# Hash attention and a squared-ReLU MLP: the last pair of the last chunk made a wide pair, gates moved to ScalarE, steps in another order

## The chip, the cores and the metric

One Trainium2 chip, one core of it. The metric is device time in microseconds (us) of the whole kernel, lower is better. All data are float32.

## The reference

Attention over 4 batches x 8 heads, 768 tokens, head size 64, in which a query sees only the keys of its own hash bucket (6 sign bits), followed by an MLP with a squared ReLU on the 3072 tokens:

```
mask   = bucket(q)[:, :, :, None] == bucket(k)[:, :, None, :]
attn   = softmax(where(mask, q @ k.T / 8, -1e9));  y = attn @ v
x      = y.transpose(0, 2, 1, 3).reshape(3072, 512)
h      = x @ w_in            # 512 -> 2048
g      = maximum(h, 0) ** 2
result = g @ w_out           # 2048 -> 512
```

## The kernel before

The first 310 us are the attention; beside it the weights are cut up and summed. Nothing of it is changed. The MLP then runs over three chunks of 1024 tokens (`i` = 0, 1, 2; the last is `NCHUNK - 1`), each with a first layer (`hidden...`) and a second (`project`). Both layers save multiplications with Winograd's form of Strassen's scheme: a product of two 2x2 block matrices is made of seven block products ("11", "21", "t1", "t2", "t3", "22", "t4") and some fifteen block sums.

The first layer of chunks 1 and 2 goes by pairs `n` = 0..3. A pair makes the 512-token columns of two rows of hidden blocks, `r0 = n` (upper) and `r = NQ + n` (lower), in the four quarters `b11`, `b12`, `b21`, `b22`; it runs as a left half (`half` 0) and a right half (`half` 1). Two forms are in use:

- `hidden_wide` (pairs 0 to 2): per half only the outer products "11" and "t2" are made whole, with 128x512 moving operands. The other five outer products, called A, D (left half), B, C, E (right half), are each cut again into seven products of 128x256 (`inner_steps`, whose `step_0` to `step_3` hold 2, 2, 2 and 1 of them).
- `hidden_pair` (pair 3): per half four outer products are whole ("11", "t1", "t2", "t3") and only A, B and C are cut again.

A float32 product is two matmul instructions on TensorE. After the products, VectorE adds the parts and either it makes the gate (`gated`, one instruction: max with 0 times itself) or ScalarE does (`gate_in`, two: Relu and Square). ScalarE also carries the products out of PSUM: `keep(acc, "one")` and `keep(acc, "two")` of the whole products, and the copies within `inner_steps`. "t2" is accumulated onto the bank that holds "11", so it can be written only after `one` was copied; in the same way each later step of A to E waits for the copy or the add that reads its bank before.

The order of all instructions is written by hand and every engine takes its own in that order (`tc.manual_schedule`). Work of a pair that is not due yet (gates, sums for the second layer) is put into the list `behind_pair` and called by `behind(m)` at fixed places of the next pair. PSUM: `acc0`, `acc1`, `acc2` with two buffers each and the two side banks `last0`, `last1`; before, the fourth product of A to D goes to a side bank.

Other names: `sums_inner` makes the right-hand sums of the cut products; `inner_sums(k)` those of the second layer's k-th outer product; `mark()` squares and adds up 768 elements per partition on ScalarE (32 such pieces, for a check of the inputs' size); `load_leaf` loads factors of the second layer (`leaf`, seven buffers), five of them ahead of `project`, on ScalarE's queue in chunks 1 and 2; `load_unit` loads the first layer's factors on SyncE's.

`project(i)` makes seven outer products k = 0..6 of seven inner ones each, all of 128x256, through `product`. In it `b11 = b22 - b_t` is made after k = 0 and `b_t = b21 - b11` after k = 2, each as two instructions of 128x2048.

Of the kernel before, what the change touches and what calls it, by code (L numbers as in the profile page):

```python
# [34 lines left out]
def kernel(  # L35
# [686 lines left out]
    def load_unit(n, pool=p_i):  # L722

        if n < NCHUNK * NR and n not in w_unit:
# [3 lines left out]
            if n < NR or pair == NQ - 1:  # L728
# [9 lines left out]
            if n >= 2 * NR:  # L738
                nc.sync.dma_start(out=five_six(w), in_=w_in_49[pair, :, 3 + half])
# [4 lines left out]
    def sum_unit(n):  # L744


        if NR <= n < 2 * NR and n % NR < NR - 2:
# [6 lines left out]
            nc.gpsimd.dma_start(out=w_in_49[pair, :, 3 + half], in_=five_six(w))  # L754
# [15 lines left out]
    with tc.manual_schedule():  # L770
# [201 lines left out]
        def product(n, w, at, bt, c11, c12, c21, c22, hook=None, last=False, beside=None, cuts=1):  # L972
# [16 lines left out]
            def keep(of, name):  # L989
                t = p_r.tile([P, 512], FP32, name=name, bufs=KEPT[name])[:, 0:w]  # L990
                nc.scalar.copy(out=t, in_=acc[of])  # L991
                return t
# [121 lines left out]
        w_inner, t_inner, spots, snaps, now, behind_pair = {}, {}, {}, {}, {}, {}  # L1114
# [77 lines left out]
        def sums_inner(i, js):  # L1192

            for j in js:
                y11, y12, y21, y22 = quarters_x(i, j)
                if j < 3:
                    tile = p_y.tile([P, NQ, QN], FP32, name=f"t{j}", **({"bufs": 2} if j < 2 else {}))
                    t = [tile[:, m] for m in range(NQ - 1)] + [y12]
                    spots[i, j] = tile[:, NQ - 1]
                else:  # L1200
# [3 lines left out]
                t_inner[i, j] = t  # L1204
# [5 lines left out]
        def inner_steps(i, j, side, w):  # L1210

            t1, t2, t4, t3 = t_inner[i, j]
            y11, _, y21, y22 = quarters_x(i, j)
            if i not in snaps:
                snaps[i] = [side_bank(m)[:, 0:QN] for m in range(2)]
            one = three = spots[i, side]
            hs = {}

            def new(unit):
                name = "five" if (j, unit) == (3, 0) else "three" if j == 4 else None
                if name:
                    return p_r.tile([P, 512], FP32, name=name, bufs=KEPT[name])
                return new_h()

            def mul(out, a, b, start, stop):
                nc.tensor.matmul(  # L1228
                    out=out, lhsT=w(a), rhs=b, start=start, stop=stop, skip_group_check=True
                )  # L1230

            def step_0():
                a0, a1 = (
                    ps_m.tile([P, 512], FP32, name=f"acc{m}")[:, 0:QN] for m in (0 if j == 4 else 1, 2)
                )
                mul(a0, 0, y11, True, False)
                nc.scalar.copy(out=one, in_=a0)
                mul(a1, 1, y21, True, True)
                hs[0] = new(0)
                nc.vector.tensor_tensor(out=hs[0][:, 0:QN], in0=a1, in1=one, op=ALU.add)  # L1240
                hs["a0"] = a0

            def step_1():
                last = hs["last"] = (
                    ps_m.tile([P, 512], FP32, name="acc2")[:, 0:QN] if j == 4 else snaps[i][side]
                )
                mul(hs["a0"], 4, t2, False, False)
                nc.scalar.copy(out=hs[0][:, QN:HN], in_=hs["a0"])
                mul(last, 3, t1, True, False)
                hs[1] = new(1)  # L1250
                nc.scalar.copy(out=hs[1][:, QN:HN], in_=last)

            def step_2():
                mul(hs["a0"], 5, t3, False, False)
                nc.scalar.copy(out=three, in_=hs["a0"])
                mul(hs["last"], 6, y22, False, True)

            def adds():
                for unit, by in (0, hs["last"]), (1, three):
                    add_in(hs[unit][:, QN:HN], by)  # L1260

            def step_3():
                mul(hs["a0"], 2, t4, False, True)
                nc.scalar.copy(out=hs[1][:, 0:QN], in_=hs["a0"])

            def put(unit, out, other):
                add_in(hs[unit], other)
                gated(out, hs[unit])

            return step_0, step_1, step_2, step_3, put, adds, hs  # L1270
# [43 lines left out]
        def hidden_wide(i, n, half):  # L1314

            r0, r = n, NQ + n
            w, acc, add, keep = outer_steps(i, n, half)
            own = own_factors(w, half)
            if half == 0:
                load_inner(i, n + 1)  # L1320
                load_third_inner(i, n + 1, nc.sync)
                now["A"] = inner_steps(i, 0, 0, w_inner[i, n][0])
                if n == 0:
                    sums_inner(i, (3,))
                now["D"] = inner_steps(i, 3, 1, lambda a: own[a])
            A, D = now["A"], now["D"]
            u0 = D[6]
            add(acc, 0, "11", True, False)
            one = keep(acc, "one")
            if half == 0:  # L1330
                A[0]()
                D[0]()
                if n == 0:
                    mark()
                    sums_inner(i, (4,))
                behind(0)
            else:
                B, C = inner_steps(i, 2, 0, w_inner[i, n][2]), inner_steps(i, 1, 1, w_inner[i, n][1])
                E = inner_steps(i, 4, 2, lambda a: own[a])
                B[0]()  # L1340
                C[0]()
                E[0]()
                A[4](1, b11[:, r], one)
                behind(2)
                sum_unit(i * NR + 2 * n + 2)
            add(acc, 4, "t2", False, True)
            two = keep(acc, "two")
            if half == 0:
                A[1]()
                D[1]()  # L1350
                A[2]()
                D[2]()
                A[3]()
                D[3]()
                if n == 0:
                    mark()
                A[5]()
                D[5]()
                add_in(u0[0], two)
                A[4](0, b11[:, r0], one)  # L1360
                sum_unit(i * NR + 2 * n + 1)
                behind(1)
                now["two"] = two
                return
            two_0 = now["two"]
            B[1]()
            C[1]()
            add_in(u0[1], two)
            B[2]()
            C[2]()  # L1370
            B[5]()
            E[1]()
            C[5]()
            B[3]()
            E[2]()
            B[4](0, b12[:, r0], u0[0])
            C[3]()
            E[3]()
            E[5]()
            B[4](1, b12[:, r], u0[1])  # L1380
            hC, hE = C[6], E[6]
            add_to(b22[:, r0], u0[0], hE[0])
            add_to(b22[:, r], u0[1], hE[1])
            add_in(two_0, hE[0])
            add_to(b21[:, r0], hC[0], two_0)
            behind(3)

            def step_0():
                gate_in(b22[:, r0])
                add_in(two, hE[1])  # L1390
                add_to(b21[:, r], hC[1], two)
                for m in r0, r:
                    minus(b_t[:, m], b12[:, m], b11[:, m])
                inner_sums(0, slice(n, n + 1))
                minus(b12[:, r0], b22[:, r0], b12[:, r0])

            def step_1():
                gate_in(b22[:, r])

            def step_2():  # L1400
                gate_in(b21[:, r0])
                minus(b12[:, r], b22[:, r], b12[:, r])

            def step_3():
                gate_in(b21[:, r])

            for m, step in enumerate((step_0, step_1, step_2, step_3)):
                behind_pair[m].append(step)

        def hidden_pair(i, n, half):  # L1410
# [3 lines left out]
            if half == 0:  # L1414
                now["A"], now["C"], now["B"] = (
                    inner_steps(i, j, (0, 0, 1)[j], w_inner[i, n][j]) for j in range(3)
                )
# [6 lines left out]
            else:  # L1424
                B[2]()
                B[5]()
                C[0]()
                A[4](1, b11[:, r], one)
                B[4](0, b12[:, r0], now["two"])
                behind(3)  # L1430
            other = ps_m.tile([P, 512], FP32, name="acc2")
# [13 lines left out]
            if half == 0:  # L1445
                A[2]()
                A[5]()
                B[0]()
                A[4](0, b11[:, r], one)
                add_in(two, five)  # L1450
            else:
                C[2]()
                C[5]()
                add_in(two, five)
                B[4](1, b12[:, r], two)
                minus(b_t[:, r], b12[:, r], b11[:, r])
                inner_sums(0, slice(n, n + 1))
                C[4](0, b21[:, r0], now["three"])
# [8 lines left out]
            else:  # L1467
# [3 lines left out]
                C[4](1, b21[:, r], three)  # L1471
# [95 lines left out]

        def project(i):
# [60 lines left out]
            for k in range(7):  # L1629
# [23 lines left out]

                def hook():
                    y21 = b[:, NQ:NR, 0:QN]
                    minus(y21, y21, t2)
                    if marks(i, k):
# [9 lines left out]
                    if k == 6 and more:  # L1667
                        load_third_inner(i + 1, 0, nc.scalar)
                        sums_inner(i + 1, (0, 1))

                counted = []

                def a_with_load(m, k=k):
# [4 lines left out]
                use = uses[k]  # L1678
                product(
                    NQ, QN, a_with_load, bt, lambda *p: use(0, *p), lambda *p: use(1, *p),  # L1680
                    lambda p: use(2, p, None), lambda *p: use(3, *p), hook,
                    (i, k) == (NCHUNK - 1, 6), mark if marks(i, k) else None,
                )
# [5 lines left out]
                if k == 0:  # L1689

                    for h in range(2):
                        at_h = slice(h * NQ, (h + 1) * NQ)
# [293 lines left out]
```

## Time and profile before

| | |
|---|---|
| median of 3 runs | 849.79 us (848.64 to 850.54) |
| profiled execution: own time / span | 851.49 us / 849.9 us |
| TensorE (PE) busy | 841.6 us, 99% |
| VectorE (DVE) busy | 758.5 us, 89% |
| ScalarE (ACT) busy | 439.8 us, 52% |
| granted TensorE clock | 0.999 |
| attention | 0 to 314 us |
| chunk 1: first layer / second | 495 to 585 / 585 to 670 us |
| chunk 2: first layer / second | 670 to 759 / 759 to 844 us |

An engine is busy from the start to the end of its instructions; matmuls are pipelined, so that the starts of successive ones (0.215 us apart) lie closer than their length (0.379 us). In a row of the timeline stand the start in us, the length, the engine, the line of the kernel, the operation and the tiles; a bracket names the idle time before it and what ended it. Line numbers in rows are those of the kernel before.

### The profile page before, as it was taken

To read this page: it belongs to the slowest core of one execution; us is meant where nothing else is said; L and a number is where in the kernel's file an instruction comes from. 1 tells how busy PE (TensorE), PEld (TensorE's weight loads), DVE (VectorE), ACT (ScalarE), POOL (GpSimd) and SP (SyncE) were. 2 spreads that over 40 slices of the span, in tenths; PEclk is the share of its full clock that TensorE was granted. 3 is DMA by queue.
4 is the path that set the end of the run, shared out by engine and by line. 5 is a ranking of instruction groups with operands and counts; after the bars stand their busy time and mean duration, and the time that the engine had idled before them with its cause. 6 is when DMAs were issued, how large, how long until landed. Compare 5 with 4: busy or idle time off the path is not lost.

```text
span 849.9 us, 17478 instructions
## 1 busy us (share of the span) xinstructions
PE 841.6 (99%) x6698; PEld 555.4 (65%) x6698; DVE 758.5 (89%) x1087; ACT 439.8 (52%) x833; POOL 171.0 (20%) x289
## 2 busy tenths in 40 slices
PE   9999999999999999999999999999999999999997
PEld 4444444444475445544788877767888777768885
DVE  4898999999999988989899989988988988888876
ACT  5887777878777762222211146775232457753210
POOL 1321121303221201643121220001211300021103
PEclk9999999999999999999999999999999999999999
DMA  9966999989996426999977994418878964157666
GB/s 185 201 130 138 185 186 201 207 173 224 249 245 202 158 69 245 330 312 306 359 254 220 275 226 145 146 50 292 298 214 244 247 207 145 51 169 213 201 166 128
DMA packets 237304, 174.10 MB, mean 205 GB/s; under 512 B 165224, under 2 KB 195248, under 8 KB 237216
## 3 DMA queue, kind: packets, MB, share of 16 engines
q1 hardware_dynamic: 196976, 90.14, 43.3%
q0 software_dynamic: 16992, 44.02, 16.5%
q10 hardware_dynamic: 23248, 38.78, 14.7%
q8 instruction: 54, 0.88, 0.5%
q14 instruction: 34, 0.28, 0.1%
HBM read 129.51 MB, written 42.73 MB: 203 GB/s over the span
## 4 chain that ended last, share of the span: by engine, by line
PE 95%; DMA 2%; DVE 1%; ACTq 0%; issue 0%; ACT 0%; POOL 0%; SPq 0%; POOLq 0%; DVEq 0%
PE acc L984 40%; PE st L478 18%; PE xo L532 14%; PE acc L1228 10%; PE acc L1298 8%; PE last L1228 3%; PE tot L589 1%; PE hash L396 1%; DMA bits<-signed 1%; DMA out_dram<-h 1%; PE tp L342 0%; DMA qk_nat<-in_q_dram 0%; ACTq L1499 0%; DVE h L1522 0%; DVE o L1288 0%
## 5 line engine op out<-in xcount | busy, mean ns | idle before, releaser
L484 ACT ACTIVATE e<-st 128x768 f32<-128x768 f32 x192 | 155.5, 810 | 56.8 <-PE st L478 52.5
L532 PE MATMUL xo<-e,v_nat 64*64 64x385 f32 (+1 forms) x1520 | 156.7, 483 | 0.0
L984 PE MATMUL acc<-b,leaf 128*128 128x256 f32 x600 | 133.1, 379 | 0.0
L984 PEld LDWEIGHTS acc<-b,leaf 128*128 128x128 f32 x600 | 113.9, 190 | 16.1 <-issue 0.5
L478 PE MATMUL st<-feat 64*64 64x384 f32 x1056 | 109.3, 483 | 0.0
L444 POOL DMA_DIRECT2D bits<-signed x120 | 62.1, 522 | 196.5 <-ACT signed L433 194.7
L532 PEld LDWEIGHTS xo<-e,v_nat 64*64 64x64 f32 (+1 forms) x1520 | 58.5, 133 | 65.7 <-issue 54.7
L984 PE MATMUL acc<-t,leaf 128*128 128x256 f32 x336 | 76.1, 379 | 0.0
L984 PEld LDWEIGHTS acc<-t,leaf 128*128 128x128 f32 x336 | 63.7, 190 | 9.1 <-issue 0.3
L478 PE MATMUL st<-bits 64*64 64x384 bf16 x768 | 65.9, 324 | 0.4 <-DMA bits<-signed 0.4
L520 DVE TENSOR_TENSOR total<-total,e 128x1536 f32<-128x1536 f32 x32 | 56.0, 1750 | 7.6 <-ACT e L484 6.9
L1028 POOL DMA_DIRECT2D raw_qk<-in_q_dram x32 | 17.3, 541 | 212.3 <-ACT raw_qk L1033 209.8
L520 DVE TENSOR_TENSOR t_x<-t_x,e 128x1536 f32<-128x1536 f32 x32 | 55.8, 1744 | 3.9 <-ACT e L484 3.8
L478 PEld LDWEIGHTS st<-feat 64*64 64x64 f32 x1056 | 39.8, 133 | 25.6 <-issue 21.7
L984 PE MATMUL acc<-x,w_unit 128*128 128x512 f32 (+1 forms) x144 | 56.5, 546 | 0.0
L984 PE MATMUL acc<-b_t,leaf 128*128 128x256 f32 x240 | 53.8, 379 | 0.0
L991 ACT COPY two<-acc 128x256 f32<-128x256 f32 (+1 forms) x29 | 12.5, 431 | 75.2 <-PE acc L984 59.7
L1076 DVE SCALAR_TENSOR_TENSOR b<-h 128x512 f32<-128x512 f32 x72 | 49.1, 691 | 2.2
L991 ACT COPY one<-acc 128x256 f32<-128x256 f32 (+1 forms) x29 | 12.5, 431 | 72.6 <-PE acc L984 53.3
L984 PEld LDWEIGHTS acc<-b_t,leaf 128*128 128x128 f32 x240 | 45.6, 190 | 6.2
L478 PE MATMUL st<-t_x 64*64 64x384 f32 x480 | 48.9, 482 | 0.0
L478 PEld LDWEIGHTS <-bits 64*64 64x64 bf16 x768 | 24.6, 107 | 35.2 <-issue 32.8
(234 smaller groups left out, 1537.8 us busy)
## 6 DMA issues: line engine op xcount, KB each, us to landing
leaf<-w_out ACTq DMA_DIRECT2D x142, 256.0 KB, 3.4
raw<-in_moe_w_in_dram SPq DMA_DIRECT2D x8, 1024.0 KB, 6.4
raw<-in_moe_w_out_dram SPq DMA_DIRECT2D x8, 1024.0 KB, 7.5
w_unit<-w_in SPq DMA_DIRECT2D x8, 896.0 KB, 8.5
w_out<-sums POOLq DMA_DIRECT2D x16, 448.0 KB, 7.4
v_nat<-in_v_dram SPq DMA_DIRECT2D x16, 384.0 KB, 5.1
x_all<-x_raw SPq DMA_DIRECT2D x16, 384.0 KB, 3.2
raw_qk<-in_q_dram POOLq DMA_DIRECT2D x32, 192.0 KB, 3.6
```

What stands on the lines that cost most here:

```text
L396: nc.tensor.matmul(out=banks[g * NR_B:(g + 1) * NR_B, h, 0:HS], lhsT=projs[rows, h * D:h * D + NR_B], rhs=feat[pr][rows, w, c * HS:(c + 1) ...
L444: nc.gpsimd.dma_start(out=t[h * D:h * D + NBITS + 1, w, c * HS:(c + 1) * HS], in_=signed[pr % 2][at:at + NBITS + 1, h],)
L478: nc.tensor.matmul(out=st[k * HK:(k + 1) * HK, h, 0:HS], lhsT=src[1][rows, key], rhs=src[0][rows, cut], start=first, stop=not first, skip_ ...
L484: nc.scalar.activation(out=key_of(pr, kt)[:, :, i, 0:HS], in_=st[:, :, 0:HS], func=ACTF.Exp, scale=scale)
L520: nc.vector.tensor_tensor(out=totals[pr], in0=totals[pr], in1=e, op=ALU.add)
L532: return nc.tensor.matmul(out=outs[pr][h * D:(h + 1) * D, c, 0:HS + 1], lhsT=nat[pr, "v_nat"][rows, h, kt * D:(kt + 1) * D], rhs=key_of(pr ...
L984: nc.tensor.matmul(out=acc[to][:, at_c], lhsT=a(i), rhs=b(i)[:, at_c], start=first and i == 0, stop=last and i == n - 1, skip_group_check= ...
L991: nc.scalar.copy(out=t, in_=acc[of])
L1028: nc.gpsimd.dma_start(out=raw_qk[i][:, w], in_=flat[:, i * n:(i + 1) * n])
L1076: nc.vector.scalar_tensor_tensor(out=out, in0=h, scalar=0.0, in1=h, op0=ALU.max, op1=ALU.mult)
L1228: nc.tensor.matmul(out=out, lhsT=w(a), rhs=b, start=start, stop=stop, skip_group_check=True)
L1298: nc.tensor.matmul(out=to, lhsT=w[:, PLACE[a], f], rhs=bt[b](f), start=first and f == 0, stop=last and f == NFT // 2 - 1, skip_group_check ...
```

## The change

- Last chunk: pair 3 is made by `hidden_wide` too (`i > 1 or s // 2 < NQ - 1`). Its factors are loaded in the wide form, and `sum_unit` makes the sums of its factors in place. What it leaves to do is not put into `behind_pair` but into `now["edge"]`: the first product (k = 0) of the last `project` calls it behind its own steps (`hook`, `early`, and `then` after the copies `two`, `five`, `three`). Three `mark()` that were in `hidden_pair` stand in its right half.
- Upper left gates: `b11[:, r0]` and `b11[:, r]` of wide pairs are gated by ScalarE (`gate_in`), and `b12[:, r]` in chunk 1 as well; before, VectorE did it (`put`).
- Steps in another order: in left halves of pairs 1 to 3, A's and D's first steps stand before "11" and their first three before "t2"; in right halves E's second step stands before C's third, and so on. `behind_pair` has six places in place of four, filled otherwise. The inner products use `acc1` and `acc2` alone (A to D) or the two side banks (E), and the second products' parts are added from PSUM on VectorE onto a copy.
- The five first leaves of chunks 1 and 2 are loaded by SyncE.
- `b11 = b22 - b_t` and `b_t = b21 - b11` are made by quarters: one quarter at the place of before, one in the hook of k = 2 and of k = 4, two in the hook of k = 3 and after k = 4.

The core of the diff:

```diff
-                (hidden_wide if s // 2 < NQ - 1 else hidden_pair)(i, s // 2, s % 2)
+                (hidden_wide if i > 1 or s // 2 < NQ - 1 else hidden_pair)(i, s // 2, s % 2)
...
-                        load_leaf(n, i == 0)
+                        load_leaf(n, True)
...
             if half == 0:
...
+                else:
+                    A[0]()
+                    D[0]()
+                    add(acc, 0, "11", True, False)
+                    behind(0)
+                    one = keep(acc, "one")
+                    behind(1)
+                    A[1]()
+                    D[1]()
+                    A[2]()
+                    D[2]()
+                    behind(2)
+                    add(acc, 4, "t2", False, True)
+                    two = keep(acc, "two")
+                now["two"] = two
+                A[3]()
+                behind(3)
+                D[3]()
+                add_in(D[4][0], two)
+                add_to(b11[:, r0], A[4][0], one)
+                behind(4)
+                gate_in(b11[:, r0])
...
+            add(acc, 0, "11", True, False)
+            one = keep(acc, "one")
+            add_to(b11[:, r], A[4][1], one)
+            B[0]()
+            C[0]()
+            E[0]()
+            behind(5)
+            gate_in(b11[:, r])
+            if edge:
+                mark()
+            add(acc, 4, "t2", False, True)
+            two = keep(acc, "two")
+            add_in(u0[1], two)
+            B[1]()
+            C[1]()
+            if edge:
+                mark()
+            B[2]()
+            E[1]()
+            if edge:
+                mark()
+            C[2]()
+            B[3]()
+            E[2]()
+            put(hB[0], b12[:, r0], u0[0])
+            C[3]()
+            E[3]()
+            add_to(b22[:, r0], u0[0], hE[0])
...
+            steps = (
+                (sums_0, gates_0), (sums_1,),
+                (sums_2, gates_1, lambda: ahead(both), gates_2),
+                (lambda: inner_sums(0, slice(n, n + 1)),), (gates_3,),
+                (lambda: over(both), gates_4),
+            )
```

`sums_0` is the rest of `b12[:, r]` and `b22[:, r]`, `sums_1` and `sums_2` those of `b21`, `gates_0` to `gates_4` the ScalarE gates of `b22[:, r0]`, `b12[:, r]` (chunk 1 alone), `b22[:, r]`, `b21[:, r0]`, `b21[:, r]`; `ahead(both)` is `b_t = b12 - b11` of both rows, `over(both)` is `b12 = b22 - b12`.

More of the change, by code (lines that the diff above doesn't have):

```diff
@@ L1328, in hidden_wide @@
+            E = inner_steps(i, 4, lambda a: own[a])
+            u0 = D[4]
             add(acc, 0, "11", True, False)
             one = keep(acc, "one")
[L1330 to L1345, printed above, removed]
+            add_to(b11[:, r], A[4][1], one)
```

279 lines of the change are left out of this document (169 added, 110 removed).

## The prediction

> **What bounds the kernel now.** I read the page first (busy times, the chain that ended last), then the windows of the eight pairs of the cut first layers, then the timeline of each engine in one pair.
>
> ```profile
> span 849.9 us, 17478 instructions
> PE 841.6 (99%) x6698; PEld 555.4 (65%) x6698; DVE 758.5 (89%) x1087; ACT 439.8 (52%) x833; POOL 171.0 (20%) x289
> PE 95%; DMA 2%; DVE 1%; ACTq 0%; issue 0%; ACT 0%; POOL 0%; SPq 0%; POOLq 0%; DVEq 0%
> 495.14:517.12 21.98, 21.98 (x88) 16.35 (x87) 18.55 (x46) 12.65 (x32) 3.27 (x6) 1.00 0.63 184
> 517.12:539.31 22.19, 22.19 (x87) 16.26 (x87) 20.81 (x47) 14.74 (x35) 1.08 (x2) 1.00 0.43 139
> 539.31:561.50 22.19, 22.19 (x88) 16.26 (x87) 19.93 (x43) 15.90 (x37) 0.54 (x1) 1.00 0.40 128
> 561.50:584.93 23.43, 23.25 (x76) 13.89 (x75) 19.78 (x37) 17.16 (x39) 3.20 (x7) 1.00 0.44 146
> 713.77:735.75 21.98, 21.98 (x87) 16.35 (x87) 19.22 (x39) 15.89 (x37) 0.00 (x0) 1.00 0.40 129
> 735.75:758.62 22.87, 22.87 (x75) 13.97 (x75) 20.25 (x38) 17.28 (x39) 2.13 (x4) 1.00 0.36 116
> ```
>
> TensorE is the chain, 95% of it. In the windows (length, then busy time of PE, PEld, DVE, ACT, POOL) a wide pair lasts 21.98 us, 22.19 twice in chunk 1, and pair 3 lasts 23.43 and 22.87. What the products themselves take is read from their starts:
>
> ```profile
> 701.11 1.88 PE L1298 MATMUL acc<-x,w_unit 128*128 128x512 f32 x4
> 702.83 1.03 PE L1228 MATMUL acc<-x,leaf 128*128 128x256 f32 x4
> 703.69 1.03 PE L1228 MATMUL acc<-x,sum 128*128 128x256 f32 x4
> 576.83 1.45 PE L1298 MATMUL acc<-t_x,w_unit 128*128 128x512 f32 x3
> 578.45 0.70 PE L1228 MATMUL acc<-t,leaf 128*128 128x256 f32 x2 [0.17 <-ACT t L1255]
> 578.99 0.38 PE L1228 MATMUL acc<-t,sum 128*128 128x256 f32 x1
> ```
>
> Four instructions of 512 take 1.72 us, four of 256 take 0.86: a product of 256 (two instructions) is 0.43 us. A wide pair has 8 products of 512 and 35 of 256: 8 x 0.86 + 35 x 0.431 = 21.97. So three of the wide pairs shown have no gap at all. A `hidden_pair` has 16 and 21: 22.81; in chunk 2 it has 0.06 us of gaps, in chunk 1 about 0.6. After a wait the first two instructions take 0.54 instead of 0.43 (578.45 to 578.99): a wait costs 0.1 beyond itself.
>
> So there is little to win: 0.90 us (22.87 to 21.97) for the last pair, 0.21 twice, 0.6 in chunk 1's pair 3, and in k = 1 of chunk 1's `project`, behind the two big `b11` sums of VectorE, about 0.2:
>
> ```profile
> 599.23 1.24 PE L984 MATMUL acc<-b,leaf 128*128 128x256 f32 x5
> 600.45 0.89 PE L984 MATMUL acc<-t,leaf 128*128 128x256 f32 x3
> ```
>
> Five starts at 0.215 end at 600.31; the next is at 600.45, and with the restart it is 0.2. Together 2.1 us. Everything else the change does is on engines beside TensorE, and counts only where TensorE comes to wait for it.
>
> **The change part by part.** The rows that give the pace of VectorE and ScalarE:
>
> ```profile
> 691.64 0.68 DVE L1273 TENSOR_TENSOR h<-h 128x512 f32<-128x512 f32 x1
> 692.36 0.69 DVE L1076 SCALAR_TENSOR_TENSOR b<-h 128x512 f32<-128x512 f32 x1
> 692.97 0.68 DVE L1288 TENSOR_TENSOR b<-five,three 128x512 f32<-128x512 f32 x1
> 693.57 0.68 DVE L1288 TENSOR_TENSOR b<-h,three 128x512 f32<-128x512 f32 x1
> 695.50 0.42 DVE L1240 TENSOR_TENSOR h<-acc,t 128x256 f32<-128x256 f32 x1
> 695.84 0.41 DVE L1240 TENSOR_TENSOR five<-acc,t 128x256 f32<-128x256 f32 x1
> 698.70 0.42 DVE L676 TENSOR_TENSOR t<-b 128x256 f32<-128x256 f32 x1
> 699.15 0.42 DVE L676 TENSOR_TENSOR t<-b,t 128x256 f32<-128x256 f32 x1
> L676 DVE TENSOR_TENSOR b<-b,t 128x1024 f32<-128x1024 f32 x10 | 12.2, 1220 | 4.8 <-PE acc L984 4.8
> 695.11 0.63 ACT L1278 ACTIVATE b<-b 128x512 f32<-128x512 f32 x1
> 695.78 0.63 ACT L1081 ACTIVATE b<-b 128x512 f32<-128x512 f32 x1
> 703.03 0.58 ACT L1309 COPY one<-acc 128x512 f32<-128x512 f32 x1 [0.15 <-PE acc L1298]
> 703.51 0.38 ACT L1237 COPY t<-acc 128x256 f32<-128x256 f32 x1
> 705.18 0.37 ACT L1237 COPY t<-acc 128x256 f32<-128x256 f32 x1 [0.49 <-PE acc L1228]
> 705.45 0.63 ACT L1278 ACTIVATE b<-b 128x512 f32<-128x512 f32 x1
> L1033 ACT ACTIVATE raw_qk<-raw_qk 128x768 f32<-128x768 f32 x32 | 27.2, 849 | 2.8 <-DMA raw_qk<-in_k_dram 1.5 <-ACT one L991 0.5
> ```
>
> From start to start VectorE takes 0.61 for 512 elements, 0.34 for 256 and (1.22 less the same overlap of 0.08) 1.14 for 1024; 0.11 more if a step needs the one just before. ScalarE: Relu to its Square 0.67; otherwise an instruction's length less 0.10, so 0.53 after a Square, 0.48 after a 512 copy, 0.27 after a 256 copy. A copy starts 0.20 after the last start interval of its product ends (702.83 to 703.03), TensorE follows a copy by 0.05 (578.02 + 0.38 to 578.45), and from VectorE to ScalarE, which no row shows alone, I take 0.06, an estimate after that 0.05.
>
> *Wide pairs of the last chunk (pairs 1 to 3).* Let a left half start at 0. TensorE needs 9.48 for it (A's and D's 14 products at 0.431, "11" and "t2" at 1.72 each), then "11" (1.72) and the first steps of B, C, E (2.59): "t2" of the right half is due at 13.79, if `one` is copied by then. On ScalarE `one` stands behind `gate_in(b11[:, r0])`, whose Relu needs VectorE's `b11` add, which is the last of this VectorE queue: E's two adds of the pair before (from -0.65; its product ends at -1.30, copied by -0.72), `put` (0.72 and 0.61), `b22[:, r0]` to 1.95, A's add; D's add waits until 2.53, as D's copy needs the single buffer `five`, which the `b22` add reads until 2.03; then 0.34, `put` 0.72 + 0.61, `b22` 0.61, `sums_1` 0.72 + 0.61 + 0.61 (to 6.73), four adds of A and D 1.34, `b21` 0.61, `ahead` 1.14, `inner_sums` 0.45 + 0.34 + 0.33, `u0` 0.61: the `b11` add runs from 11.55 to 12.23. Relu 12.29, Square 12.96, `one` 13.49 to 14.07, "t2" at 14.12: 0.33 late, 0.43 with the restart. Then ScalarE's own queue: copies of B, C, E and two gates (0.48 + 3 x 0.27 + 0.67 + 0.53 + 0.67 + 0.53) put `two` at 17.18 and B's next copy at 17.66 to 18.03; B's third step, due at 17.67, starts at 18.08: 0.41 + 0.10. Per pair 0.94; pairs 1 and 2 together 1.9.
>
> *Pair 3 of the last chunk.* The same, but a `mark` (0.85, and 0.1 for reading its sum) stands ahead of `two`: B's step waits 1.37 + 0.10, and C's last step 0.33 behind the third mark. With the 0.43: 2.2.
>
> *Pair 0 of both chunks.* VectorE makes E's right-hand sums ahead of the `b11` add, which ends at 12.02: `one` to 13.87, "t2" 0.24 late. Twice: 0.5.
>
> *Pairs 1 and 2 of chunk 1.* `b12[:, r]` is one add there in place of `put`: the queue is 0.72 shorter, "t2" is in time; `two` is at 16.46, B's copy at 17.32, its step 0.12 + 0.10 late: 0.22 each, where 0.21 each goes away (its cause, factor sums ahead of C's add, is behind another step now). Nil.
>
> *Pair 3 of chunk 1.* The leaf loads leave ScalarE; in its place four activations (`gates_1`, `gates_2`) stand ahead of the right half's `one`: `one` at 14.50 instead of 13.56, B's copy to 15.36, its two adds to 16.18, and "t1", whose bank is now the one these adds free, starts at 16.23 instead of 15.08: 1.25, for the 0.6 that goes.
>
> *First product of the last `project`.* `three` is copied behind `b22`'s gates and a mark, at 10.05 to 10.42; "t4" is due at 10.34: 0.2.
>
> *At nothing.* Leaf loads on SyncE: queued behind `load_unit`, which waits for the left half to end, they still land 3.4 us after issue,
>
> ```profile
> leaf<-w_out ACTq DMA_DIRECT2D x142, 256.0 KB, 3.4
> ```
>
> with the right half (some 11 us) as cover; without it, up to 3.4 us. The quarters: the same elements, 2.3 us of them moved behind k = 4, where VectorE's idle time takes most; if not, the next chunk's D waits for its sums, 0 to 1.4 us in two places.
>
> Sum: 1.9 + 2.2 + 0.5 + 1.25 + 0.2 = 6.05 (pairs 1 and 2 of chunk 1 cancel their 0.4) against 0.9 + 0.6 + 0.2 = 1.7: about +4.3. I take +4.1, as D's wait of 0.25 is the step that I know least. The span would be 854.0. The profiled execution took 851.49 for a span of 849.9, and the median is 849.79; the difference goes onto the median: **853.9 us**, for this case 852 to 856.
>
> The Trainium skill ("ScalarE: Activation LUTs", Rules for kernel authors) says that relu, max and mul belong on VectorE rather than ScalarE. The rows agree: 0.69 as one step against 0.63 + 0.63. By that rule the `b11` gates would stay and `one` would stand behind nothing of VectorE's: the first two terms would be about 1 instead of 4.1.
>
> **Rivals.**
> - *The gate is in time.* If VectorE's queue is 0.95 us shorter than I add up, neither "t2" nor B's step waits, and marks find room. For it: ScalarE is 52% busy, VectorE would be about 80% in a pair. Against: the queue is added up from rows whose spacings recur within 0.01 us, and two of its members (D's copy, the `put`) cannot go anywhere else. The 2.1 us come out: 847.7.
> - *Half in time* (0.5 shorter): the first wait goes, B's step waits 0.4 in three pairs, pair 3 of chunk 1 costs as it did before: about +0.9, 850.7.
> - *VectorE drags into the next chunk* through the moved quarters, deciding where it enters a chunk over 1.6 us later than before: up to 1.4 twice on top, and at the upper end a leaf late: 856.5.
> - That the wide pair is not run for pair 3 is ruled out: in the order of the instructions that pair has five cut products.
>
> **How the numbers follow.** Forecast 0.55, gate in time 0.13, half in time 0.19, drag 0.13. A measurement of this kernel tells 0.2% (1.7 us) from no change: slower 0.68, same 0.19, faster 0.13. The range, 848.6 to 856.8, leaves out most of the fast case and the end of the drag.
>
> **What would show it.** Right: waits of TensorE for `one` (L1321) and for B's copy (L1258) in pairs 1 to 3 of the last chunk, those pairs at 22.9, 22.9 and 24.2 us, `b11`'s Relu waiting for VectorE just before `one`; pair 3 of chunk 1 at 24.1. Wrong: those pairs at 22.0, with `one` copied before 13.7 us of the pair.

## The result, and the profile after

The changed kernel takes **856.1 us** (median of 4 runs, 855.68 to 856.5), the kernel before 849.78 beside it: a ratio of 1.0075, 95% interval 1.0058 to 1.0093. It is slower by 6.3 us; forecast was 4.1. Rows below carry the line numbers of the kernel that they come from. In the kernels after, L1310 are the products of 512 and L1242 the cut ones, L1321 is `keep`, L1252 to L1276 are the copies of the cut products, L1285 and L1300 VectorE's adds, L1290 and L1084 the Relu and the Square of `gate_in`.

The page of the kernel after, in the order of the prediction's first fence: the span, the busy times, the chain that ended last.

```profile
span 855.0 us, 17532 instructions
PE 843.3 (99%) x6710; PEld 563.8 (66%) x6710; DVE 748.3 (88%) x1081; ACT 458.1 (54%) x868; POOL 170.9 (20%) x289
PE 89%; DVE 4%; ACT 3%; DMA 2%; issue 1%; ACTq 0%; POOL 0%; DVEq 0%; POOLq 0%
```

VectorE has 10 us less to do, ScalarE 18 more, and the chain, 95% TensorE before, now runs 7% through these two. The windows of the eight pairs after (length, then busy time of PE, PEld, DVE, ACT, POOL), chunk 1 first:

```profile
496.31:519.56 23.25, 22.68 (x87) 16.02 (x86) 17.77 (x49) 13.93 (x34) 3.44 (x7) 1.00 0.66 183
519.56:541.80 22.24, 22.24 (x87) 16.26 (x86) 18.72 (x43) 17.98 (x42) 1.08 (x2) 1.00 0.43 139
541.80:564.04 22.24, 22.24 (x87) 16.26 (x86) 17.91 (x39) 17.97 (x42) 0.54 (x1) 1.00 0.42 128
564.04:588.65 24.61, 23.14 (x75) 13.90 (x74) 20.17 (x37) 17.17 (x39) 3.04 (x6) 1.00 0.42 139
673.26:695.44 22.18, 22.18 (x88) 16.19 (x87) 14.86 (x37) 13.83 (x34) 2.69 (x6) 1.00 0.76 219
695.44:718.24 22.80, 22.50 (x87) 16.17 (x86) 17.57 (x36) 16.80 (x40) 0.00 (x0) 1.00 0.41 135
718.24:741.06 22.82, 22.51 (x88) 16.18 (x86) 18.40 (x40) 16.81 (x40) 0.00 (x0) 1.00 0.40 125
741.06:764.99 23.93, 22.80 (x88) 16.01 (x87) 18.15 (x39) 18.93 (x46) 2.13 (x4) 1.00 0.35 116
```

Against the pairs of before (21.98, 22.19, 22.19, 23.43; in chunk 2 21.98 three times and 22.87) these are +1.27, +0.05, +0.05, +1.18, +0.20, +0.82, +0.84, +1.06: 5.5 us. With 0.41 at the end of chunk 0's `project` (waits and restarts, row below), and 0.2 saved in k = 1 of chunk 1's, that is 5.7.

The same number comes from the ends. From the first matmul of the first layer (314.06 before, 314.90 after) to the end of the last matmul of the run (844.29 and 850.84) it is 530.24 before and 535.94 after: **+5.70 us**. I call this length the *stretch* below. It leaves out the attention, which began its last part 0.85 later in this execution, and the stores at the end, which took 1.45 less. Over the 14 traces of this study, with an attention that no kernel changes, the stretch starts anywhere from 312.94 to 314.90, so a difference of one microsecond between two single times says little, and one between two stretches says more. It is not free of chance either: where a load lands late, a wait of some tenths comes and goes.

Who ends TensorE's waits after, without the attention's rows and that of the last output (waits view: us in total, times, longest):

```profile
PE acc L1242 <- ACT h L1258: 1.5, 3, 1.1
PE acc L1310 <- DVE h L1285: 1.5, 1, 1.5
PE acc L1242 <- ACT h L1261: 0.5, 1, 0.5
PE acc L985 <- issue: 0.2, 1, 0.2
```

The first is B's copy in the last chunk's pairs, the second `t1` of chunk 1's pair 3, both of which the prediction named; the third and fourth stand where nothing was priced. The first of them in the timeline, pair 1 of the last chunk, which starts at 695.44:

```profile
706.92 0.68 DVE L1300 TENSOR_TENSOR b<-h,one 128x512 f32<-128x512 f32 x1
707.63 0.63 ACT L1290 ACTIVATE b<-b 128x512 f32<-128x512 f32 x1 [0.95 <-DVE b L1300]
708.29 0.63 ACT L1084 ACTIVATE b<-b 128x512 f32<-128x512 f32 x1
708.36 1.03 PE L1242 MATMUL last<-t_x,w_unit 128*128 128x256 f32 x4
708.83 0.57 ACT L1321 COPY one<-acc 128x512 f32<-128x512 f32 x1
709.45 1.98 PE L1310 MATMUL acc<-t_x,w_unit 128*128 128x512 f32 x4
712.50 0.57 ACT L1321 COPY two<-acc 128x512 f32<-128x512 f32 x1
712.96 0.38 ACT L1258 COPY h<-acc 128x256 f32<-128x256 f32 x1
713.39 1.13 PE L1242 MATMUL acc<-x,leaf 128*128 128x256 f32 x4 [0.23 <-ACT h L1258]
```

ScalarE stands idle 0.95 us for VectorE's `b11` add, then makes Relu and Square, and only then copies `one`, whose product has long been done; "t2" starts 0.05 behind the copy. The row of "t2" names no wait at all: by the starts of the matmuls before it (four from 708.36, 0.216 apart, end at 709.22) it is 0.23 late, and its own restart costs 0.10 (a length of 1.98, where the prediction's row at 701.11 has 1.88 for four such matmuls). Short waits are seen in starts, not in brackets.

The third stands in pair 0 of chunk 1, which starts at 496.31, and the fourth, the first row here, at the end of chunk 0's `project`:

```profile
494.51 1.97 PE L985 MATMUL acc<-b_t,leaf 128*128 128x256 f32 x8 [0.17 <-issue]
501.05 0.71 DVE L1600 STREAM_TRANSPOSE h<-o 128x512 f32<-128x512 f32 x1
501.69 0.38 DVE L1285 TENSOR_TENSOR h<-h,acc 128x256 f32<-128x256 f32 x1
502.77 0.88 DVE L676 TENSOR_TENSOR o<-t_x,o 128x256 f32<-128x256 f32 x2
502.86 0.37 ACT L1261 COPY h<-acc 128x256 f32<-128x256 f32 x1 [0.33 <-PE acc L1242]
503.34 0.89 PE L1242 MATMUL acc<-o,w_unit 128*128 128x256 f32 x3 [0.51 <-ACT h L1261]
```

VectorE is still at chunk 0's last outputs until 501.69; the add that reads A's bank comes 5.4 us into the pair. Before, it was through with the outputs at 497.98, 2.8 us into a pair that started at 495.14, and went on to D's right-hand sums:

```profile
497.98 0.38 DVE L676 TENSOR_TENSOR o<-t_x 128x256 f32<-128x256 f32 x1
```

So it enters the chunk 2.5 us later, and the second steps of A and D wait, by the starts 0.32 and 0.75 with their restarts. The bracket of D's step names a copy of A's product, only because it ended last (503.23). By the program D's step does not need that copy. It needs the second of D's right-hand sums, the first of the two instructions at 502.77, which took 0.42 and ended at 503.19.

### The profile page after: what moved, and what is told of

Its sections match the earlier page's. It is cut to its first block, busy times and chain, and to the rows that moved or that the text cites. A ratio compares the mean times of both kernels' runs of the same rounds, so it can differ in the third digit from the quotient of the medians.

```text
span 855.0 us, 17532 instructions
## 1 busy us (share of the span) xinstructions
PE 843.3 (99%) x6710; PEld 563.8 (66%) x6710; DVE 748.3 (88%) x1081; ACT 458.1 (54%) x868; POOL 170.9 (20%) x289
## 4 chain that ended last, share of the span: by engine, by line
PE 89%; DVE 4%; ACT 3%; DMA 2%; issue 1%; ACTq 0%; POOL 0%; DVEq 0%; POOLq 0%
PE acc L985 41%; PE st L478 17%; PE xo L532 14%; PE acc L1242 8%; PE acc L1310 5%; PE last L1242 2%; DMA bits<-signed 2%; PE tot L589 1%; PE hash L396 1%; DVE b L1300 1%; DVE h L1285 1%; ACT b L1084 1%; ACT b L1290 1%; DVE b_t L676 1%; DVE five L1285 0%
## 5 line engine op out<-in xcount | busy, mean ns | idle before, releaser
L532 PE MATMUL xo<-e,v_nat 64*64 64x385 f32 (+1 forms) x1520 | 158.5, 483 | 0.0
L532 PEld LDWEIGHTS xo<-e,v_nat 64*64 64x64 f32 (+1 forms) x1520 | 62.5, 133 | 61.7 <-issue 49.9
L478 PE MATMUL st<-bits 64*64 64x384 bf16 x768 | 68.0, 324 | 1.5 <-DMA bits<-signed 1.5
L478 PEld LDWEIGHTS <-bits 64*64 64x64 bf16 x768 | 26.5, 107 | 34.9 <-issue 32.7
L985 PEld LDWEIGHTS acc<-x,w_unit 128*128 128x128 f32 x144 | 27.3, 190 | 26.6 <-issue 24.9
```

The source lines that it names most:

```text
L478: nc.tensor.matmul(out=st[k * HK:(k + 1) * HK, h, 0:HS], lhsT=src[1][rows, key], rhs=src[0][rows, cut], start=first, stop=not first, skip_ ...
L532: return nc.tensor.matmul(out=outs[pr][h * D:(h + 1) * D, c, 0:HS + 1], lhsT=nat[pr, "v_nat"][rows, h, kt * D:(kt + 1) * D], rhs=key_of(pr ...
L985: nc.tensor.matmul(out=acc[to][:, at_c], lhsT=a(i), rhs=b(i)[:, at_c], start=first and i == 0, stop=last and i == n - 1, skip_group_check= ...
```

## The experiments

All are edits of the changed kernel. Ratios are against the kernel before on the same chip, with their 95% interval; 0.001 is 0.85 us.

**1. Gates back on VectorE** (`gates_vector`)

```
-  add_to(b11[:, r0], A[4][0], one)  ...  gate_in(b11[:, r0])
+  put(A[4][0], b11[:, r0], one)
-  add_to(b11[:, r], A[4][1], one)   ...  gate_in(b11[:, r])
+  put(A[4][1], b11[:, r], one)
```

> The changed kernel with both gates of b11 in the wide pairs back on VectorE (add and one gating step, as put does), nothing else. Theory (ScalarE's queue: `one`, `two` and B's copy stand behind those gates): the waits for `one` (0.10 to 0.24 us, plus 0.10 for the restart) and for B's copy (0.16 in pairs 1 and 2 of chunk 1, 0.39 in pairs 1 and 2 of the last chunk, 1.2 in its pair 3, plus 0.10 each) go: 2 x 0.83 + 1.66 + 2 x 0.20 + 2 x 0.26 = 4.2 us less than the changed kernel's 856.1, so 851.9. Rival (VectorE is as full as ScalarE: 0.72 us more for each half of a pair): the same waits come back as TensorE's wait for VectorE's adds in D or for `five`, 0.5 us or more a pair, and the time stays at 855 to 858. Rival (the loss lies outside the wide pairs): 856.1 within 0.5, though the two waits are gone from the trace.

1.0020 (1.0009 to 1.0030), stretch 531.59: 4.35 less than the changed kernel. The last chunk's pairs 1 to 3 in the windows of this kernel:

```profile
693.91:715.89 21.98, 21.98 (x88) 16.34 (x86) 18.84 (x38) 15.15 (x36) 0.00 (x0) 1.00 0.44 141
715.89:737.86 21.97, 21.97 (x87) 16.34 (x86) 19.67 (x42) 15.16 (x36) 0.00 (x0) 1.00 0.41 129
737.86:759.84 21.98, 21.98 (x88) 16.34 (x86) 19.42 (x41) 17.01 (x42) 2.14 (x4) 1.00 0.38 126
```

No wait is left in any of them, pair 3 with its three marks included, though VectorE is busy 1.3 us more in each. The theory holds, and the rival that VectorE is the bound falls. In pair 0 of chunk 1 the waits of A and D stay, and E waits 0.34 with its restart.

**2. Position or amount** (`one_first`, `both_later`). In the first, only the left half's gate goes behind the right half's `one`; in the second the right half's gate goes to the end of the pair as well. ScalarE's work is the same in all three kernels.

```
one_first:
-  gate_in(b11[:, r0])        (left half, end)
   one = keep(acc, "one")     (right half)
+  gate_in(b11[:, r0])
both_later, besides:
-  gate_in(b11[:, r])         (right half, ahead of "t2")
+  gate_in(b11[:, r])         (end of the pair; in the last pair behind E[2]())
```

> The changed kernel with one call moved: the gate of the left half's b11 stands behind the copy `one` of the right half instead of ahead of it. ScalarE does the same work. Theory (position: `one` waits because the Relu ahead of it waits for VectorE): the waits for `one` go, 0.24 + 0.10 in pairs 1 to 3 of the last chunk and 0.10 + 0.10 in pair 0 of both chunks, 1.4 us in all; the waits for B's copy stay within 0.1 of 0.16, 0.39 and 1.2, as the gate ends where it did: 854.7. Rival (amount: ScalarE's work between the gate and B's copy sets the place where TensorE waits): the first waits go, B's copy waits for their sum (0.7 to 0.8 in pairs 1 and 2 of the last chunk), and the time stays at 856.1.

> As the run before, and the gate of the right half's b11 moved too, from ahead of `two` to the end of the pair (in the last pair: to behind E's third step). ScalarE does the same work, none of it between `one` and B's copy but copies, older gates and the marks. Theory (position): both kinds of wait go, 2 x 0.83 + 1.66 + 2 x 0.20 + 2 x 0.26 = 4.2 us: 851.9. Rival (amount): the gates are then ahead of the next pair's first copies of A and D, whose banks TensorE needs 1.7 us later, and waits of 0.3 to 0.5 appear there in up to six pairs: 854 to 855.

`one_first`: 1.0045 (1.0029 to 1.0061), stretch 533.53, 2.4 less where 1.4 was expected. The waits for `one` go, and those for B's copy fall too, from 0.39 to 0.25 in pairs 1 and 2 of the last chunk and from 0.16 to 0.04 in chunk 1, since ScalarE now copies `one` while it would have stood idle for VectorE. `both_later`: 1.0019 (1.0008 to 1.0029), stretch 531.82, 4.1 less; pair 3 keeps two restarts of 0.10, and 0.3 of waits appears in the project stages. So it is the place of the gates in ScalarE's queue that costs, not their being ScalarE's: moved behind the copies they cost no more than on VectorE. That they would hold up the next pair is not seen.

**3. The quarters** (`whole_sums`, `whole_first`). The project's second sum (`b11 = b22 - b_t`) and its fourth (`b_t = b21 - b11`) are made whole again, each as two instructions of 128x2048: in all chunks, or in chunk 0 alone. Shown for the second sum; the fourth likewise.

```
-  second_sum(*Q21), (*Q11), (*Q22), (*Q12) at k = 2, 3, 3, 0
+  for h in range(2): minus(b11[:, at_h], b22[:, at_h], b_t[:, at_h])   at k = 0
```

> The changed kernel with the second and fourth sum of the project stage whole again, behind k = 0 and k = 2 as in the kernel before. Theory (drag: the quarters moved behind k = 3 and 4 leave VectorE late at the start of the next chunk): the waits at the end of chunk 0's project (0.33 + 0.08 us) and in pair 0 of chunk 1 (0.22 + 0.10 and 0.68 + 0.07) go, 1.5 us, and 0.2 comes back in k = 1 of chunk 1: 854.8. Rival (the drag is made by the new order of the steps in pair 0, not by the sums): the waits stay where they are, 0.2 comes back, 856.3.

> The changed kernel with the second and fourth sum whole in chunk 0's project only; chunks 1 and 2 keep the quarters. Theory (the quarters do two things: in chunk 0 they leave VectorE late for the next chunk's pair 0, in the last chunk they give VectorE room in k = 0 to 2, where the last pair's own sums now stand): the waits at the end of chunk 0 and in pair 0 of chunk 1 go (0.38 + 0.32 + 0.75 us), nothing comes back in chunk 2: 1.45 less than the changed kernel, from the first matmul of the first layer to the last matmul of the run 534.5 instead of 535.9. Rival (whole sums cost wherever they stand): 0.35 comes back in k = 1 of chunk 0, and pair 0 of chunk 1 still waits 0.3: 535.6.

`whole_sums`: 1.0087 (1.0069 to 1.0104), stretch 537.06, not 1.3 less but 1.1 more. The waits at the end of chunk 0 and of A and D in chunk 1's pair 0 are gone, as the theory says (0.20 is left there), and 0.35 comes back in chunk 1's project. But in the last chunk a new wait stands, which neither theory had:

```profile
778.53 4.48 DVE L676 TENSOR_TENSOR b<-b,b_t 128x2048 f32<-128x2048 f32 x2
786.46 1.22 DVE L676 TENSOR_TENSOR b<-b,t 128x1024 f32<-128x1024 f32 x1
787.77 1.97 PE L985 MATMUL acc<-b,leaf 128*128 128x256 f32 x8 [2.09 <-issue]
```

The sum of 4.48 us is made behind the last pair's own left-over sums, which the change has moved into k = 0, and the next product waits 2.25 + 0.08 for the sum at 786.46, which stands behind it. So the quarters do pay in the last chunk of this kernel, where the wide pair 3 leaves its sums to k = 0. `whole_first`, whole sums in chunk 0 only, confirms it: 1.0050 (1.0036 to 1.0064), stretch 534.38, 1.57 less than the changed kernel, and nothing comes back.

**4. The last pair narrow** (`narrow_last`), cut as before; its factors are loaded in the narrow form, too. Its `t1` and `t3` read other values than the reference's, and so its output is not the reference's: the changed kernel writes a sum of the cut products over a quarter of their right-hand sides, which a wide pair no longer reads. The instructions and their sizes are those of the narrow pair.

```
-  hidden_wide if i > 1 or s // 2 < NQ - 1 else hidden_pair
+  hidden_wide if s // 2 < NQ - 1 else hidden_pair
```

> The changed kernel with the last chunk's pair 3 cut as before (three cut products instead of five), all else as changed. Theory (the wide pair saves 0.86 us of TensorE and pays 0.34 + 1.32 + 0.28 of waits): the pair gets 0.9 longer and 1.9 of waits go, so 1.0 less, 534.9 us from the first layer's first matmul to the last of the run instead of 535.9, if the pair's left-over steps find the room that they had before. Rival (the hidden pair has the same left-over gates ahead of `one` as chunk 1's pair 3, and waits 1.73 for the bank of `t1` as that one): 0.9 + 1.73 - 1.94 = 0.7 more, 536.6.

1.0074 (1.0058 to 1.0091), stretch 535.92: no difference in all. In the pair itself the theory holds: its waits are 0.28 and 0.08 in place of 1.95, and "t1" does not wait 1.73, so the rival falls. What it saves, 0.8, is in this execution lost in pairs 0 and 1 of chunk 1 (0.71 and 0.12): there VectorE waits 4.05 us for a load of factors where the changed kernel's trace has 3.07, and its sums of these factors come later. That stands before the edit. In `gates_vector` and `pair3_gates` TensorE waits at the same place, 0.34 and 0.66. That the narrow pair is better by itself is likely and not shown by the times.

**5. Pair 3 of chunk 1** (`pair3_gates`, `side_bank`). What "t1" waits for, in the kernel after:

```profile
577.45 1.23 DVE L676 TENSOR_TENSOR b_t<-b,b 128x1024 f32<-128x1024 f32 x1 [1.58 <-ACT b L1084]
579.32 0.69 DVE L1079 SCALAR_TENSOR_TENSOR b<-h 128x512 f32<-128x512 f32 x1
580.26 0.75 DVE L1285 TENSOR_TENSOR h<-h,acc 128x256 f32<-128x256 f32 x2
580.73 1.55 PE L1310 MATMUL acc<-t_x,w_unit 128*128 128x512 f32 x3 [1.47 <-DVE h L1285]
```

VectorE waits 1.58 for the Square of `b12`'s gate, makes `b_t`, the gating sum of `b22`, and then reads B's banks, the first of which `t1` takes. Two ways out were tried: the left-over steps later, or another bank.

```
pair3_gates:
   B[1]()                    (left half)
-  behind(2)
   C[0]()                    (right half)
+  behind(2)
side_bank:
-  other = ps_m.tile([P, 512], FP32, name="acc2")
+  other = side_bank(0)
```

> The changed kernel with one call moved in chunk 1's pair 3: the third list of left-over steps (a sum, the gates of b12 and b22, the sum b_t, 1024 wide) runs in the right half behind C's first step instead of in the left half ahead of its last gating sum. Theory (those gates and the b_t sum that waits for them delay `one`, and with it B's adds that free the bank of `t1`): the wait of `t1`, 1.63 + 0.10 us, goes, and at most 0.3 appears at `t3`: 1.4 to 1.7 less than the changed kernel, 534.3 us from the first layer's first matmul to the last one of the run instead of 535.9. Rival (the bank: `t1` takes the bank that B's adds free whatever stands ahead): the wait shrinks by the two gates on ScalarE, 0.94, and 0.7 stays: 535.0. Second rival: the sum of 1.14 ahead of `put` moves the wait to `t2` or `t3`: no gain.

> The changed kernel with one word moved: in chunk 1's pair 3 the product `t1` accumulates in a side bank, free since the pair before, instead of in the bank that B's adds free. Theory (the bank: `t1` waits only because VectorE reads B's banks late, and nothing else needs those adds so early): the wait of 1.63 + 0.10 us goes and none above 0.2 appears in the pair; 534.2 us from the first layer's first matmul to the last of the run, where the changed kernel has 535.9. Rival (ScalarE's queue, which holds six activations in this stretch): the wait moves to B's or C's third step and to `t3`, as it did when the gates were moved, and 535.5 or more stays.

`pair3_gates`: 1.0087 (1.0072 to 1.0103), stretch 538.17, no gain. That is the second rival's outcome, but it came about otherwise. "t1" waits 0.18, and C's third step and `t3` wait in its stead, for ScalarE's copies, 2.05 with the restarts where it was 1.81:

```profile
584.51 1.13 PE L1242 MATMUL acc<-x,sum 128*128 128x256 f32 x4 [0.78 <-ACT h L1258]
586.10 1.12 PE L1310 MATMUL acc<-t_x,w_unit 128*128 128x512 f32 x2 [0.45 <-ACT two L1321]
```

Eight activations in a row, 578.60 to 583.44, now stand ahead of `five` and of C's copy. The pair thus costs 0.24 more. The other 2.0 of the longer stretch lie outside it: 0.7 in chunk 0's project and 0.8 in pairs 0 and 1 of chunk 1, ahead of the edit, and 0.6 in chunk 1's project, where a leaf lands late. `side_bank`: 1.0049 (1.0032 to 1.0066), some 2.2 us less than the changed kernel's ratio, though the two intervals overlap. "t1" starts at once, nothing in the pair waits over 0.08, and the theory of the bank holds for the pair. The stretch (536.24) is not the 534.2 of this theory: the profiled execution, the slowest of the six, gives the gain back outside the pair, 0.7 in chunk 0's project, ahead of the edit, and 1.4 in chunk 1's, right behind it, where it waits for leaves (the last section says why). From its timeline:

```profile
579.46 1.88 PE L1310 MATMUL last<-t_x,w_unit 128*128 128x512 f32 x4
598.18 5.94 PE L985 MATMUL acc<-b,leaf 128*128 128x256 f32 x24 [0.17 <-DMA leaf<-w_out]
```

**6. The marks** (`marks_out`): the last pair's three go into project stages.

```
-  if edge: mark()                                       (three times)
+  marks at (i, k) = (0, 6), twice, and one more at (1, 0)
```

> The changed kernel with the three squares of queries and keys (marks) of the last pair done in project stages instead, two in chunk 0's last product and one in chunk 1's first; 32 in all as before. Theory (a mark ahead of `two` and one behind C's step make the last pair's waits larger than those of pairs 1 and 2): its wait for B's copy falls from 1.22 to 0.4 and the two short ones of 0.10 go, 1.0 us less than the changed kernel: 534.9 us from the first layer's first matmul to the last. Rival (the gates alone decide, a mark fits into ScalarE's idle time behind them): the wait stays above 1.0, 535.9.

1.0067 (1.0050 to 1.0084), stretch 536.38. Pair 3's wait for B's copy falls from 1.22 to 0.40 and the two restarts behind it go, as the theory says: a mark ahead of `two` costs its whole length (0.82 of 0.83). The microsecond came back, 1.27 with the restart, where I had put the third mark:

```profile
601.96 0.84 ACT L1036 ACTIVATE raw_qk<-raw_qk 128x768 f32<-128x768 f32 x1 [5.69 <-DMA raw_qk<-in_k_dram]
603.35 0.37 ACT L992 COPY one<-acc 128x256 f32<-128x256 f32 x1
603.78 2.43 PE L985 MATMUL acc<-t,leaf 128*128 128x256 f32 x10 [1.00 <-ACT one L992]
```

The loads of marks are two ahead, so three marks close together wait for a load, and ScalarE's copies wait behind them: the same mechanism again, with a DMA in VectorE's place.

**7. Repairs together** (`combo_scalar`: `both_later`, `whole_first`, `pair3_gates`; `combo_bank`: with `side_bank` in place of the last; `combo_vbank`: the same with `gates_vector` in place of the first).

> Four repairs in one: b11's gates stay on ScalarE but behind `one` and at the end of the pair, whole sums in chunk 0, and in chunk 1's pair 3 the left-over steps behind C's first step. Theory (the waits are separate and add up): from 535.9 us between the first layer's first matmul and the last of the run go 4.1, 1.45 and 1.6: 528.8, where the kernel before has 530.24; 1.4 us faster than before, ratio 0.998. Rival (VectorE and ScalarE are full, and each wait that goes moves to the next place): at least half of the last two gains is lost, 530.3 or more, no faster than before.

> Three repairs in one: b11's gates on ScalarE but behind `one` and at the end of the pair, whole sums in chunk 0, `t1` of chunk 1's pair 3 in the side bank. Theory (separate waits that add up): 535.9 less 4.1, 1.45 and 1.7 is 528.6 us from the first layer's first matmul to the last, where the kernel before has 530.24; 1.6 us faster than before, ratio 0.998. Rival (a wait comes back in chunk 1's pair 3 or in the project stage behind it): 530 or more, the same as before.

> The run before with b11's gates on VectorE instead of later on ScalarE. Theory (either way of taking the gates from ahead of `one` and `two` is worth the same): 528.0 to 528.6, ratio 0.998. Rival (VectorE, 0.72 us longer in every half, becomes the bound in some pair): waits for VectorE's adds of 0.3 or more, 529.5 or more.

| | ratio | 95% interval | median, us | before beside it | stretch, us |
|---|---|---|---|---|---|
| changed kernel | 1.0075 | 1.0058 to 1.0093 | 856.1 | 849.78 | 535.94 |
| `combo_scalar` | 0.9998 | 0.9987 to 1.0008 | 849.79 | 850.17 | 530.39 |
| `combo_bank` | 0.9988 | 0.9978 to 0.9998 | 849.29 | 849.85 | 529.29 |
| `combo_vbank` | 0.9984 | 0.9973 to 0.9995 | 848.78 | 849.85 | 529.43 |

The waits are separate and nearly add up: what the single repairs measured (4.1 and 1.6 less, 0.2 more for `pair3_gates`) gives 530.5 for `combo_scalar`. Its own expectation, 528.8, counted on a gain of `pair3_gates` that is not there; 2.05 is left in chunk 1's pair 3, and it equals the kernel before. The other two beat both kernels, by 0.12% and 0.16% against before, at the edge of what can be told. They are 0.7 and 0.8 to 1.4 us short of what was expected, nearly all of it in chunk 1's project: without the wait of `t1` TensorE arrives there 1.7 us earlier, and waits for leaves, 0.8 and 1.1 in all.

## Why the prediction was right or wrong

The direction and the main cause were right. 856.1 lies inside the range, but just above the 852 to 856 of the forecast's own case and nearer to the drag rival's 856.5. The time was 2.2 us short, of which 1.6 lies in the terms (5.7 against 4.1) and the rest in what single executions differ by. That the terms are out by no more than this is in part luck: the last chunk's pairs 1 to 3 came out 0.5 below (3.6 for 4.1) and `t4` 0.2, while chunk 1's pair 3 came out 0.5 above and 1.5 was not priced at all.

- **Pairs 1 and 2 of the last chunk, 0.94 each: 0.82 and 0.84, right.** From the pair's start the `b11` add ran 11.48 to 12.16 (worked out: 11.55 to 12.23), Relu at 12.19 (12.29), `one` at 13.39 (13.49), "t2" at 14.01 (14.12), B's third step at 17.95 (18.08). The queue of 24 VectorE steps was added up to within 0.1 us. D's wait, for which the forecast took 0.2 off its sum, came as worked out: D's add starts 2.49 us into the pair (2.53). Experiments 1 and 2 show that the gates' place is the cause.
- **Pair 3, 2.2: 1.95, right.** A wait of 0.24 for "t2", 1.22 for B's copy and 0.07 behind the third mark, with four restarts of 0.10. Of the wait for B's copy the mark makes 0.82 (experiment 6).
- **Pair 0, 0.24 twice: 0.20 in both chunks, right.** In chunk 1 the quarters add 1.07, see below.
- **Chunk 1's pairs 1 and 2, nil: +0.05 each, right.** The new wait is 0.16 + 0.10, the old one is gone.
- **Chunk 1's pair 3, 1.25 for 0.6: 1.73 and 0.08, mis-sized by 0.5.** The bank was the right one, but the working followed only ScalarE's queue (`one`, then B's copy). VectorE had a queue of its own there, `b_t` held up 1.58 by the Square and the gating sum behind it, and that ended later. With the bank changed the wait is gone.
- **"t4" behind `three` in the last project, 0.2: no wait**, the products of k = 0 follow each other at 0.215 throughout.
- **Gains 0.9, 0.6, 0.2: right**; without the gates the wide pair 3 takes 21.98 for 22.87, and k = 1 of chunk 1's project has no gap. One reading is off: of the four wide pairs in the prediction's first fence two, not three, are without a gap.
- **The quarters, priced at nothing: wrong, the step that failed.** "VectorE's idle time takes most" left out how late VectorE already was at the end of a project. Behind k = 4 of chunk 0 it had no idle time to give: it entered chunk 1 2.5 us later than before, where the rival had put the point at 1.6, and TensorE waited 0.41 at the end of chunk 0 and 0.75 + 0.32 in pair 0. That is the drag rival (0.13), in one of its two places, by the wait that the prediction had named for it: D waits for its sums. `whole_first` prices it at 1.57 us. The prediction also missed what the quarters are worth in the last chunk, 2.3 us.
- **Leaf loads on SyncE, at nothing:** no wait of the changed kernel's stretch is for a leaf; the loads were not tried by themselves.

The rule that the prediction took from the Trainium skill ("ScalarE: Activation LUTs", Rules for kernel authors), relu, max and mul on VectorE, held here by more than I gave it: with the gates there, pairs 1 to 3 wait not about 1 us but not at all (windows of experiment 1). Experiment 2 limits it: on ScalarE behind the copies the gates cost the same.

## What to carry to other kernels

An engine with time to spare still runs its queue in order: before a step is moved to it, ask what the step waits for and which copies stand behind it; here gates of 1.2 us each, on an engine 52% busy before, cost 4 us in all because they stood ahead of two copies, and no more than on VectorE once they stood behind them. Work that is put off "into idle time" has to be followed to the next place where its engine is late, for each chunk separately: the same quarters cost 1.6 us in one chunk and saved 2.3 in another. When a wait is taken out, look at what the engine then reaches sooner, and at the engines that do not get there sooner with it.

## What the runs showed of the hardware

The last point, the waits for leaves, is made by a queue and by the DMA engines together. The part of chunk 1's project where the repaired kernels wait, in the windows of `combo_vbank` (the last two numbers are the DMA engines' share and GB/s):

```profile
590.37:596.37 6.00, 5.72 (x26) 4.43 (x26) 5.86 (x9) 1.58 (x4) 1.06 (x2) 1.00 1.03 403
```

Its leaf loads in this part of the project (588 to 603 us), and later in the same project (612 to 665), with count, size and median us from issue to landing:

```profile
leaf<-w_out ACTq DMA_DIRECT2D x8, 256.0 KB, 6.9
leaf<-w_out ACTq DMA_DIRECT2D x28, 256.0 KB, 3.1
```

All sixteen DMA engines are busy (share 1.03) at 403 GB/s, as the next chunk's inputs, 2 MB issued by GpSimd, are loaded at the same time; a leaf lands 6.9 us after its issue instead of 3.1. The Trainium skill ("DMA: Bandwidth & Descriptors", Issuing engines are not separate DMA queues) says that transfers issued by different engines end up on the same sixteen DMA engines and interleave; the trace agrees.

That alone does not make TensorE wait. The changed kernel loads the same things there, its leaves take as long (7.6 us, 588 to 603), and it waits for none. What differs is the project's first leaf on ScalarE's queue. The first line is the changed kernel's, whose project starts at 588.65; the others are `combo_vbank`'s, whose project starts at 584.37:

```profile
588.93 0.33 ACTq L1577 DMA_DIRECT2D leaf<-w_out  x1
585.12 0.37 ACT L1276 COPY h<-acc 128x256 f32<-128x256 f32 x1 [0.40 <-DVE h L1285]
585.23 0.33 ACTq L1575 DMA_DIRECT2D leaf<-w_out  x1
593.41 6.90 PE L985 MATMUL acc<-b,leaf 128*128 128x256 f32 x28 [0.24 <-DMA leaf<-w_out]
```

These two loads by themselves, in the same order (windows 588.7 to 589.2 and 584.9 to 585.4):

```profile
leaf<-w_out ACTq DMA_DIRECT2D x1, 256.0 KB, 5.0
leaf<-w_out ACTq DMA_DIRECT2D x1, 256.0 KB, 8.0
```

TensorE reaches the project sooner, and VectorE not by as much: its add that this copy waits for starts 1.5 us ahead of the project in the changed kernel (587.17) and 0.25 us into it here (584.62). So a copy of ScalarE waits 0.40 us, and the load behind it goes out 0.86 us into the project in place of 0.28. It takes 8.0 us in place of 5.0 and lands between 593.2 and 593.3; TensorE's first wait ends at 593.41. `side_bank` and `combo_bank` issue that leaf at 0.85, too. So the gates' story comes back once more, with a DMA issue in the place of the copy. That 0.6 us at the issue make 3 us at the landing because the 2 MB, issued 0.15 us into the project, come to stand ahead is argued only. Neither an earlier issue of this leaf nor a later load of the inputs was tried.
